# Which early pieces of K and Q take the float32 path through the SP and ACT queues: the third instead of the second

## The chip, the cores and the metric

The kernel runs on one core of a Trainium2 chip. The metric is the device time of one execution in microseconds (us), lower is better; a kernel's time is the median of several runs. Five runs of the kernel before gave 302.68, 302.68, 301.27, 301.18 and 304.01 us.

The engines go by these names: PE is TensorE (matmuls and transposes), ACT is ScalarE, DVE is VectorE, POOL is GpSimd, and SP is SyncE, which only issues transfers. SP and ACT issue transfers through hardware queues (q1 and q10 in the profile), POOL through a software queue (q0), which can change the type of the data on the way.

## The reference

Sliding-window attention over 8 batches of 8 heads, and then a two-layer block with a squared ReLU on all 4608 tokens:

```python
B, H, S, D = 8, 8, 576, 64
scores = (q @ k.T) / sqrt(D)                    # per batch and head, S x S
mask = abs(pos[:, None] - pos[None, :]) <= 32   # window of 32 to both sides
attn = softmax(where(mask, scores, -1e9))
x = (attn @ v), heads side by side              # 4608 x 512
h = x @ w_in                                    # 512 -> 2048
out = (relu(h) ** 2) @ w_out                    # 2048 -> 512, float32
```

Inputs and the output are float32; the kernel computes in bf16 with float32 accumulation.

## The kernel before, in words

**Attention.** Queries go in chunks of 64 tokens (9 for each batch, numbered n = 0 to 71), each against the 128 keys around it. Q and K come in as rows of tokens; PE transposes them against an identity matrix into PSUM, and DVE (K, line 505) and ACT (Q, line 502) copy the result into `KT` and `QT`. Then, for a group of chunks: scores on PE (line 585), the exponential on ACT (605), the mask on DVE (614), attention times V on PE (720 and 721), a reciprocal and a scaling on DVE (731, 733), a transpose of the result on PE (749), and a copy into `XT` on ACT (755). For odd chunks V is needed at another offset, so DVE copies V from `VX` to `VD` (543).

**The block after it.** `mm1` multiplies `XT` by `w_in` (lines 768, 791, 809), ACT applies the ReLU, DVE squares, and `mm2` multiplies by `w_out` (861). The first token tile uses `mm1_small`, which needs 128 tokens and a quarter of `w_in`. The first one needs chunks 0 and 1 in `XT` and the quarter called w10.

**Loading batch 0.** Its tokens come in six pieces, `PIECE0 = ((0, 96), (96, 64), (160, 128), (288, 128), (416, 128), (544, 32))`, as (first token, count). Piece x of K is called k0x here, of Q q0x, of V v0x (V has five pieces of its own). Pieces 0 and 1 of K and Q come by `first_load` (line 454): a plain float32 copy, K on SP's queue and Q on ACT's, into the staging tiles that `STG` names. Piece 0 goes into two of the `OE` tiles, piece 1 into `PF`, 128 partitions of 1040 float32 elements, K at element 0 and Q at element 512. PE transposes them as float32, against a float32 identity `IDF`. All other pieces come by `tok_load` (line 461) on POOL's queue, which casts them to bf16 on the way, and are transposed as bf16. V comes by `vx_load` (531), also on POOL; weights by `load_w1` and `load_w2` (548, 553), on POOL too. The order on POOL's queue is the list `ORDER`, written by hand.

POOL also makes an index pattern with `iota` (line 413). DVE builds the two identities and the masks from it (lines 415 to 426).

**The order on every engine.** The builder records each operation with the tiles that it reads and writes, an assumed duration and a key. A list scheduler in `Prog` orders them by keys and by what an estimate of the course makes of them; keys at or below -100 hold as written. That order is fixed when the program is built, and each engine runs its list strictly in order. A transfer's assumed time is `move`: a count, a time for each, and an allowance at the end.

**Idle matmuls.** Where the scheduler's estimate leaves PE without work in the first part, `fill` puts in matmuls of a zero tile (line 410), which keep PE active; they wait for nothing but must be run through. They stop at `idle_end`, the transposes of piece 3.

The transposes of a piece are in `tok_turn`; which PSUM tiles they use depends on the piece: `HT` (the two tiles of `mm1`) or the score banks B and D.

Of the kernel before, what the change touches and what calls it, by code (L numbers as in the profile page):

```python
# [8 lines left out]
BF16 = mybir.dt.bfloat16  # L9
# [9 lines left out]
VE = D_ + 1  # L19
# [11 lines left out]
PADS, MARGINS, ROUNDS, NREP = (0, 1000, 2000), (0, 4000, 8000), 3, 4  # L31
LATE = {"POOL": 1500, "SP": 2000, "ACT": 2000}
DEPTH, POST, BACK = 4000, {"POOL": 1500, "SP": 1000, "ACT": 1000}, {"POOL": 2500, "SP": 4000, "ACT": 4000}
ORDER = ("v00 v01 k02 q02 v02 w10 k03 q03 v03 k04 q04 v04 w11 w12 w13 k05 q05 k10 q10 v10 k11 q11 v11 "
         "w20 w21 w22 w23 k12 q12 v12 k13 q13 v13 k14 q14 v14").split()
GT0, WT0 = (12.5, 16, 20, 25.5), (13, 18, 23, 26)
TURN0 = {1: 1, 2: 2, 4: 3, 6: 4}
# [321 lines left out]
class Gen:  # L359
# [5 lines left out]
    def alloc(self):  # L365
        nc = self.nc
        sb, ps = nc.alloc_sbuf_tensor, nc.alloc_psum_tensor
        self.SC = ps("sc", [128, 2048], F32)
        self.BK = {x: self.SC[:, 512 * i:512 * i + 512] for i, x in enumerate("ACBD")}
        self.TRP = self.BK["D"].bitcast(BF16)  # L370
        self.HT = [ps(f"ht{i}", [128, 512], F32) for i in range(2)]
        self.OUTP = [ps(f"outp{i}", [128, 512], F32) for i in range(2)]

        self.RAW = {t: [sb(f"{t}raw{i}", [128, 2560], BF16) for i in range(2)] for t in "qk"}
        self.QT = [sb(f"qt{i}", [128, 4, S_], BF16) for i in range(2)]
        self.KT = [sb(f"kt{i}", [128, 4, KW], BF16) for i in range(2)]
        self.VD = [sb(f"vd{i}", [128, 4, H_, VS], BF16) for i in range(2)]
        self.KA = [sb(f"ka{i}", [128, 4, 3, 128], BF16) for i in range(2)]
        self.VX = [sb(f"vx{i}", [128, 5, H_, VS], BF16) for i in range(2)]
        self.MASK = sb("mask", [128, 64], BF16)  # L380
        self.MASK2 = sb("mask2", [128, 2, 64], BF16)
        self.IOTA = sb("iota", [128, 256], mybir.dt.int32)
        self.IDW = sb("identw", [128, 256], BF16)
        self.ID = self.IDW[:, 64:192]
        self.MK = sb("mk", [128, 64], F32)
        self.E = sb("e", [128, 2048], BF16)
        self.PT = sb("pt", [128, 3 * 768], BF16)
        self.RS = [sb(f"rs{i}", [128, 16], F32) for i in range(4)]
        self.XR = sb("xr", [128, 4, 512], BF16)
        self.PF = sb("pf", [128, 16 * VE], F32)  # L390
        self.XT = sb("xt", [128, 4, NTOK], BF16)
        self.W1 = sb("w1", [128, 4, DFF], BF16)
        self.W2 = sb("w2", [128, 16, DM], BF16)
        self.GT = [sb(f"gt{i}", [128, 16, 512], BF16) for i in range(2)]
        self.RT = [sb(f"rt{i}", [128, 512], BF16) for i in range(4)]
        self.ZZ = sb("zz", [128, 128], BF16)
        self.OE = [sb(f"oe{i}", [128, 512], F32) for i in range(4)]
        self.STG = {("k", 0): (self.OE[0], 0, 512, ("oe", 0)), ("q", 0): (self.OE[1], 0, 512, ("oe", 1)),
                    ("k", 1): (self.PF, 0, 16 * VE, ("pf", 0)), ("q", 1): (self.PF, 512, 16 * VE, ("pf", 1))}
        self.IDF = self.OE[3][:, 0:128]  # L400


# [8 lines left out]

    def setup_masks(self, key):
        self.p.rec("POOL", lambda e: e.iota(self.IOTA[:], [[1, 256]], base=0, channel_multiplier=-1), writes=["iota"],
                   key=-198.5, dur=400)
        self.p.rec("DVE", lambda e: e.tensor_scalar(self.IDF, self.IOTA[:, 0:128], 0.0, None, ALU.is_equal),
                   reads=["iota"], writes=[("oe", 3)], key=key - 0.1, dur=200)
        self.p.rec("DVE", lambda e: e.tensor_scalar(self.IDW[:], self.IOTA[:], 64.0, None, ALU.is_equal),
                   reads=["iota"], writes=["id"], key=key, dur=330)
        self.p.rec("DVE", lambda e: e.tensor_scalar(self.MK[:], self.IOTA[:, 0:64], -64.0, None, ALU.is_ge),
                   reads=["iota"], writes=["mk"], key=key + 0.1, dur=130)  # L420
        self.p.rec("DVE", lambda e: e.scalar_tensor_tensor(self.MASK[:], self.IOTA[:, 0:64], 0.0, self.MK[:], ALU.is_le,
                                                           ALU.mult),
                   reads=["mk", "iota"], writes=["mask"], key=key + 0.1, dur=130)
        self.p.rec("DVE", lambda e: e.tensor_scalar(self.MASK2[:, 0, :], self.IOTA[:, 0:64], -64.0, None, ALU.is_le),
                   reads=["iota"], writes=[("mask2", 0)], key=-20, dur=130)
        self.p.rec("DVE", lambda e: e.tensor_scalar(self.MASK2[:, 1, :], self.IOTA[:, 0:64], 0.0, None, ALU.is_ge),
                   reads=["iota"], writes=[("mask2", 1)], key=-20, dur=130)
# [21 lines left out]
    def first_load(self, t, x, eng, key):  # L449
        t0, n = PIECE0[x]  # L450
        src = (self.q if t == "q" else self.k)[0, :, t0:t0 + n, :].rearrange("h p d -> p h d")
        stg, o, w, tag = self.STG[t, x]
        dst = bass.AP(stg, o, [[w, n], [64, 8], [1, 64]])
        self.p.rec(eng, lambda e: e.dma_start(dst, src), writes=[tag], dma=(f"s{t}{x}", 0), key=key, dur=420, move=(n // 2, 14, 1500))

    def tok_load(self, b, t, x, key):
        t0, n = self.pieces(b)[x]
# [8 lines left out]
    def tok_turn(self, b, x, key):  # L466
        t0, n = self.pieces(b)[x]
        early = b == 0 and x < 3
        first = b == 0 and x < 2
        if b == 0 and x == 1:  # L470
            parts = [(t, "s" + u, self.BK[u]) for t, u in ("kB", "qD")]
        elif early:
            parts = [(t, ("ht", u), self.HT[u][:] if first else self.HT[u][:].bitcast(BF16)) for u, t in enumerate("kq")]
        elif b:
            u = "DB"[x % 2]
            ps = self.BK[u].bitcast(BF16)
            parts = [("k", "s" + u, ps[:, 0:512]), ("q", "s" + u, ps[:, 512:1024])]
        elif x == 5:
            parts = [("k", "sD", self.TRP[:, 0:512]), ("q", "sD", self.TRP[:, 512:1024])]
        else:  # L480
            parts = [(t, ("outp", u), self.OUTP[u][:].bitcast(BF16)) for u, t in enumerate("kq")]

        def f(e, todo):
            for t, tag, ps in todo:
                for j in range(4):
                    stg, o, w, _ = self.STG[t, min(x, 1)]
                    src = bass.AP(stg, o + 128 * j, [[w, n], [1, 128]]) if first else bass.AP(
                        self.RAW[t][b % 2], self.slot(b, x) + 128 * j, [[2560, n], [1, 128]])
                    mm = e.transpose(ps[:, 128 * j:128 * j + n], src, self.IDF[0:n, 0:n] if first else self.ID[0:n, 0:n])  # L489
            return mm  # L490

        for todo in ([parts[:1], parts[1:]] if early else [parts]):
            rd = [self.STG[t, x][3] for t, _, _ in todo] + [("oe", 3)] if first else [("fraw", b, t, x) for t, _, _ in todo]
            self.p.rec("PE", lambda e, a=todo: f(e, a), reads=rd + ["id"],
                       writes=sorted({tag for _, tag, _ in todo}), key=key, dur=450 if first else 240 * len(todo), att=True)
        if b == 0 and x == 3:
            self.p.idle_end = self.p.ops[-1]
        for t, tag, ps in parts:
            src = ps[:, 0:512].rearrange("p (j q) -> p j q", j=4)[:, :, 0:n]
            dst = self.KT[b % 2][:, :, 32 + t0:32 + t0 + n] if t == "k" else self.QT[b % 2][:, :, t0:t0 + n]  # L500
            if b == 0 and x < 5 and t == "q":
                self.p.rec("ACT", lambda e, d=dst, c=src: e.activation(d, c, ACTF.Copy), reads=[tag], writes=[(t, b % 2, x)],
                           old=self.was(b, t, x), key=key, dur=200 + 2.8 * n, att=True)
            else:
                self.p.rec("DVE", lambda e, d=dst, c=src: e.tensor_copy(d, c), reads=[tag], writes=[(t, b % 2, x)],
                           old=self.was(b, t, x), key=key, dur=60 + 3.2 * n, att=True)
# [388 lines left out]
    def build(self):  # L895
# [18 lines left out]
        for b in range(B_):  # L914
# [2 lines left out]
                tile += 1  # L917
            if b < FB:
                if not b:
                    for x in range(2):  # L920
                        self.first_load("k", x, "SP", -300 + x)
                        self.first_load("q", x, "ACT", -300 + x)
                for bb in range(0 if b else FB):
# [15 lines left out]
            for c in range(NCH):  # L939
                n = NCH * b + c  # L940
# [33 lines left out]
                if c % 2 and not b:  # L974
                    x = (c + 1) // 2
# [6 lines left out]
                gi, k, m = self.group[n]  # L982
# [48 lines left out]
```

## Time and profile before

| | |
|---|---|
| median of 5 runs | 302.68 us (301.18 to 304.01) |
| the profiled execution's own time | 302.68 us |
| its span in the trace | 300.9 us |
| PE busy | 295.7 us, 98% of the span |
| DVE, ACT, POOL busy | 59%, 53%, 35% |
| POOL's software queue q0 | 114144 packets, 18.03 MB |
| mean granted TensorE clock | 0.994 |

The profile comes from one execution. Its span begins with the first instruction and ends with the last; 1.8 us of the execution's time lie outside of it. Times in it are microseconds from the start of the span. A line number is that of the instruction in the code above. PE and PEld are the two halves of TensorE's work, the streaming of the moving operand and the loading of the stationary one. The granted clock is the share of full speed that the hardware let TensorE run at.

### The profile page before, as it was taken

The numbers are of one execution on the slowest core, as the hardware profiler recorded it, in microseconds if no ns is written. First come the engines' busy times: TensorE is split into PE (matmuls) and PEld (weight loads), VectorE is DVE, ScalarE is ACT, GpSimd is POOL, SyncE is SP. The second block draws the span as 40 slices with busy tenths as digits, with TensorE's granted clock in tenths as the row PEclk, the third lists the DMA queues.
The fourth block names the chain that finished last, engine by engine and source line by source line (L and its number), as shares of the span: only waits on it lengthen the run. The fifth ranks groups of instructions, "written<-read, shape, count | busy, mean of one in ns | idle before, by whom it ended". The sixth has DMA issues, their size and how long they took to land.

```text
span 300.9 us, 7075 instructions
## 1 busy us (share of the span) xinstructions
PE 295.7 (98%) x2793; PEld 174.0 (58%) x2793; DVE 176.8 (59%) x429; ACT 160.1 (53%) x267; POOL 105.9 (35%) x131
## 2 busy tenths in 40 slices
PE   7989999999999999999999999999999999999996
PEld 7879955866768754444444454444444444444445
DVE  6676656764989856757665596768447663222200
ACT  2457644565758645654565665557364554444411
POOL 8999941241615531452154544316410000000000
PEclk9799999999999999999999999999999999999999
DMA  9999999999999999999799999999992210100022
GB/s 139 173 197 170 206 171 191 139 158 188 173 146 141 131 195 133 130 137 160 149 112 127 157 171 158 127 173 90 180 150 77 83 26 35 37 35 36 35 83 93
DMA packets 166817, 39.21 MB, mean 130 GB/s; under 512 B 157824, under 2 KB 162304, under 8 KB 166784
## 3 DMA queue, kind: packets, MB, share of 16 engines
q0 software_dynamic: 114144, 18.03, 88.4%
q1 hardware_dynamic: 46000, 11.02, 24.8%
q10 hardware_dynamic: 6640, 9.70, 10.0%
q8 instruction: 22, 0.36, 0.5%
q14 instruction: 11, 0.09, 0.1%
HBM read 36.70 MB, written 9.44 MB: 153 GB/s over the span
## 4 chain that ended last, share of the span: by engine, by line
PE 96%; DMA 2%; DVE 0%; ACT 0%; issue 0%; SPq 0%
PE outp L861 41%; PE ht L809 28%; PE ht L768 7%; PE ht L791 7%; PE sc L585 4%; PE sc L645 3%; DMA pf<-in_k_dram 2%; PE outp L410 2%; PE sc L489 1%; PE sc L837 1%; PE outp L837 1%; PE sc L720 0%; PE sc L693 0%; PE sc L721 0%; PE outp L749 0%; PE ht L489 0%
## 5 line engine op out<-in xcount | busy, mean ns | idle before, releaser
L861 PE MATMUL outp<-w,gt 128*128 128x512 bf16 x560 | 136.0, 379 | 0.0
L809 PE MATMUL ht<-xt,w 128*128 128x512 bf16 x384 | 94.5, 379 | 0.0
L824 DVE TENSOR_TENSOR gt<-rt 128x512 bf16<-128x512 bf16 x144 | 59.2, 419 | 58.3 <-ACT rt L815 51.1
L815 ACT ACTIVATE rt<-ht 128x512 bf16<-128x512 f32 x96 | 57.3, 598 | 56.8 <-PE ht L809 54.8
L861 PEld LDWEIGHTS outp<-w,gt 128*128 128x128 bf16 x560 | 52.7, 98 | 58.2
L809 PEld LDWEIGHTS ht<-xt,w 128*128 128x128 bf16 x384 | 36.5, 98 | 42.3
L461 POOL DMA_DIRECT2D qraw<-in_q_dram x39 | 34.0, 872 | 50.7 <-PE ht L809 24.4
L461 POOL DMA_DIRECT2D kraw<-in_k_dram x39 | 34.2, 876 | 44.3 <-PE ht L809 19.2
L605 ACT ACTIVATE e<-sc 128x512 bf16<-128x512 f32 (+1 forms) x48 | 37.4, 809 | 12.4 <-PE sc L585 12.4
L531 POOL DMA_DIRECT2D vx<-in_v_dram x40 | 35.2, 879 | 20.6 <-PE ht L809 8.5
L868 ACT ACTIVATE oe<-outp 128x512 f32<-128x512 f32 x35 | 20.9, 598 | 26.6 <-PE outp L861 26.6
L669 DVE TENSOR_TENSOR xr<-pf,rs 128x512 bf16<-128x512 f32 (+1 forms) x42 | 27.7, 682 | 0.4
L626 DVE TENSOR_TENSOR pt<-e,mask 128x512 bf16<-128x512 bf16 x42 | 17.6, 422 | 14.0 <-ACT e L605 13.9
L768 PE MATMUL ht<-xt,w 128*128 128x128 bf16 x384 | 24.1, 219 | 0.3 <-ACT xt L755 0.3
L791 PE MATMUL ht<-xt,w 128*128 128x256 bf16 x192 | 23.5, 273 | 0.0
L768 PEld LDWEIGHTS ht<-xt,w 128*128 128x128 bf16 x384 | 21.7, 98 | 0.8 <-ACT xt L755 0.5
L662 DVE COPY pf<-sc 128x520 f32<-128x520 f32 x21 | 14.7, 699 | 11.6 <-PE sc L645 11.6
L791 PEld LDWEIGHTS ht<-xt,w 128*128 128x128 bf16 x192 | 18.0, 98 | 3.3
L776 ACT ACTIVATE rt<-ht 128x512 bf16<-128x512 f32 x24 | 14.2, 599 | 10.4 <-PE ht L768 10.1
L659 ACT ACTIVATE pf<-sc 128x520 f32<-128x520 f32 x21 | 12.6, 602 | 11.9 <-PE sc L645 11.9
L797 ACT ACTIVATE rt<-ht 128x512 bf16<-128x512 f32 x24 | 14.4, 600 | 7.3 <-PE ht L791 6.8
L664 DVE TENSOR_TENSOR pf<-pf 64x520 f32<-64x520 f32 x21 | 14.6, 697 | 5.9 <-ACT pf L659 4.9
(84 smaller groups left out, 197.2 us busy)
## 6 DMA issues: line engine op xcount, KB each, us to landing
out_dram<-oe ACTq DMA_DIRECT2D x35, 256.0 KB, 3.7
kraw<-in_k_dram POOLq DMA_DIRECT2D x31, 128.0 KB, 5.2
qraw<-in_q_dram POOLq DMA_DIRECT2D x31, 128.0 KB, 5.3
vx<-in_v_dram POOLq DMA_DIRECT2D x24, 128.0 KB, 5.1
w<-in_moe_w_in_dram POOLq DMA_DIRECT2D x4, 512.0 KB, 9.6
w<-in_moe_w_out_dram POOLq DMA_DIRECT2D x4, 512.0 KB, 15.9
vx<-in_v_dram POOLq DMA_DIRECT2D x16, 96.0 KB, 5.6
xt<-xr SPq DMA_TRANSPOSE x36, 4.2
```

Source lines behind the costliest of these rows:

```text
L461: self.p.rec("POOL", lambda e: e.dma_start(dst, src), writes=[("fraw", b, t, x)], old=[("fraw", b - 2, t, y + (b == 2))], reads=self.pace( ...
L531: self.p.rec("POOL", lambda e: e.dma_start(self.VX[b % 2][r:r + n, s, :, 0:64], self.v[b, :, t0:t0 + n, :].rearrange("h p d -> p h d")), w ...
L605: self.p.rec("ACT", lambda e, d=dst, a=src: e.activation(d, a, ACTF.Exp, scale=0.125), reads=["s" + x for x in name], writes=[("e", h)], k ...
L626: self.p.rec("DVE", lambda e, a=pt, c=ee, d=mb: e.tensor_tensor(a, c, d, ALU.mult), reads=[("e", k // 2), "mask"], writes=[("ptt", k)], ol ...
L669: self.p.rec("DVE", lambda e, w=w, np=np: e.tensor_tensor(bass.AP(self.XR, 512 * (2 * y + w), [[2048, np], [64, 2], [128, 4], [1, 64]]), b ...
L768: mm = e.matmul(ht[:, 128 * (d % 4):128 * (d % 4) + 128], self.W1[:, ft, 128 * d:128 * d + 128], self.XT[:, ft, t0:t0 + 128], start=(ft == ...
L791: mm = e.matmul(ht[:, 256 * (d % 2):256 * (d % 2) + 256], self.W1[:, ft, 128 * d:128 * d + 128], self.XT[:, ft, 64 * s0:64 * s0 + 256], st ...
L809: mm = e.matmul(ht[:], self.W1[:, ft, 128 * d:128 * d + 128], self.XT[:, ft, 512 * T:512 * T + 512], start=(ft == 0), stop=(ft == 3))
L815: self.p.rec("ACT", lambda e: e.activation(rt[:], ht[:], ACTF.Relu), reads=[("ht", k % 2)], writes=[("rt", k % 4)], key=key, dur=560)
L824: self.p.rec("DVE", lambda e: e.tensor_tensor(g, r, r, ALU.mult), reads=[("rt", k % 4)], writes=tags, key=key, dur=430)
L861: mm = e.matmul(op, gt[:, d, 128 * u:128 * u + 128], self.W2[:, d, :], start=(d == 0), stop=(d == 15))
L868: self.p.rec("ACT", lambda e: e.activation(oe[:], op, ACTF.Copy), reads=[tag], writes=[("oe", x % 4)], key=key, dur=560)
```

## The change

Piece 2 (128 tokens) takes the place of piece 1 (64 tokens) on the float32 path: `first_load` is called for pieces 0 and 2, and the staging tile `PF` holds piece 2. Piece 1 now comes as bf16 through POOL, and is put first there. The `iota` gets the key of the masks, which sets it ahead of all of POOL's transfers; before, it stood behind the first one (v00). The allowance for the landing of the float32 piece 2 in the scheduler's estimate is 2500 ns instead of 1500 ns.

```diff
-ORDER = ("v00 v01 k02 q02 v02 w10 k03 q03 v03 k04 q04 v04 w11 w12 w13 k05 q05 k10 q10 v10 k11 q11 v11 "
+ORDER = ("k01 q01 v00 v01 v02 w10 k03 q03 v03 k04 q04 v04 w11 w12 w13 k05 q05 k10 q10 v10 k11 q11 v11 "
          "w20 w21 w22 w23 k12 q12 v12 k13 q13 v13 k14 q14 v14").split()
...
         self.STG = {("k", 0): (self.OE[0], 0, 512, ("oe", 0)), ("q", 0): (self.OE[1], 0, 512, ("oe", 1)),
-                    ("k", 1): (self.PF, 0, 16 * VE, ("pf", 0)), ("q", 1): (self.PF, 512, 16 * VE, ("pf", 1))}
+                    ("k", 2): (self.PF, 0, 16 * VE, ("pf", 0)), ("q", 2): (self.PF, 512, 16 * VE, ("pf", 1))}
...
         self.p.rec("POOL", lambda e: e.iota(self.IOTA[:], [[1, 256]], base=0, channel_multiplier=-1), writes=["iota"],
-                   key=-198.5, dur=400)
+                   key=key, dur=400)
...
-        self.p.rec(eng, lambda e: e.dma_start(dst, src), ..., move=(n // 2, 14, 1500))
+        self.p.rec(eng, lambda e: e.dma_start(dst, src), ..., move=(n // 2, 14, 1500 if x == 0 else 2500))
...
-        first = b == 0 and x < 2
+        first = b == 0 and x in (0, 2)
         if b == 0 and x == 1:
-            parts = [(t, "s" + u, self.BK[u]) for t, u in ("kB", "qD")]
+            parts = [(t, "s" + u, self.BK[u].bitcast(BF16)) for t, u in ("kB", "qD")]
...
-                    stg, o, w, _ = self.STG[t, min(x, 1)]
+                    stg, o, w, _ = self.STG[t, x if first else 0]
...
-                    for x in range(2):
+                    for x in (0, 2):
                         self.first_load("k", x, "SP", -300 + x)
                         self.first_load("q", x, "ACT", -300 + x)
```

The scheduler answers with another order at the start. The columns show PE's list up to the transposes of piece 3, "fill" being idle matmuls; from there on PE's list is the same in both.

| before | after |
|---|---|
| 34 fill, transposes k00, 2 fill, q00, 2 fill | 34 fill, transposes k00, 2 fill, q00, 11 fill |
| k01, 2 fill, q01, 2 fill (float32) | scores 0, 1 fill |
| scores 0, 11 fill, scores 1 | k01, 1 fill, q01, 1 fill (bf16) |
| k02 (bf16), av 0, q02 (bf16), 14 fill | k02, q02 (float32), scores 1, av 0, 14 fill |
| av 1, scores 2 and 3, 12 fill | scores 2 and 3, 2 fill, av 1, 15 fill |
| transpose of chunks 0 and 1, 12 fill | transpose of chunks 0 and 1, 2 fill |
| av 2, 2 fill, av 3, 4 fill | av 2, 2 fill, av 3, 11 fill |
| first `mm1_small`, 14 fill, k03, q03 | first `mm1_small`, 18 fill, k03, q03 |

On DVE the copy of k02 stands ahead of the first two V copies (line 543) after the change, where before three V copies stood ahead of it; on ACT the first exponential now stands ahead of the copy of q01, and the copy of q02 ahead of the second exponential.

## Prediction

> **What bounds the kernel now.** I read the chain that ended last first, then PE's waits.
>
> ```profile
> PE 96%; DMA 2%; DVE 0%; ACT 0%; issue 0%; SPq 0%
> PE outp L410 <- DVE zz L404: 1.0, 1, 1.0
> PE sc L489 <- DMA pf<-in_k_dram: 0.8, 1, 0.8
> PE outp L749 <- DVE kt L505: 0.5, 1, 0.5
> PE ht L768 <- ACT xt L755: 0.3, 1, 0.3
> ```
>
> The chain is PE but for one transfer, `pf<-in_k_dram`: k01, which the change touches. The waits (total, times, longest) all lie before 20 us; asked again for 22.3 to 299 us, the view names none. From the scores at 22.27 PE works through a fixed list. So the change is worth what it moves the start of that list by. Next, PE in order of time (start, length), up to there:
>
> ```profile
> 5.44 0.85 PE L489 MATMUL ht<-oe 96*128 96x96 f32 x4
> 7.34 0.46 PE L489 MATMUL sc<-oe,pf 64*128 64x64 f32 x4 [0.84 <-DMA pf<-in_k_dram]
> ...
> 8.56 0.29 PE L585 MATMUL sc<-qt,kt 64*128 64x64 bf16 x8
> ...
> 11.13 1.70 PE L410 MATMUL outp<-zz 128*128 128x128 bf16 x14
> ...
> 16.05 1.06 PE L768 MATMUL ht<-xt,w 128*128 128x128 bf16 x16
> 16.94 0.94 PE L410 MATMUL outp<-zz 128*128 128x128 bf16 x14
> 17.73 0.39 PE L489 MATMUL outp<-identw,kraw 128*128 128x128 bf16 x4
> ```
>
> k01 ends a wait at 7.34; the first `mm1_small` runs at 16.05, k03 is transposed at 17.73. The 14 idle matmuls at 11.13 take 0.107 us each, those at 16.94 0.056. The reason is the granted clock (columns: stretch, length, PE busy, clock, DMA share, GB/s):
>
> ```profile
> 6.38:9.79 3.41, 2.51 (x41) 1.00 2.24 163
> 9.79:13.20 3.41, 3.41 (x46) 0.50 1.77 181
> 13.20:16.60 3.40, 3.40 (x78) 1.00 2.39 161
> ```
>
> Half clock for 3.41 us, right after a stretch in which PE was busy for 2.51 of 3.41 us. Last the transfers: two issues (KB, us to landing), then the packets of 4.0 to 5.4 us, when hardware and software queues share:
>
> ```profile
> pf<-in_k_dram SPq DMA_DIRECT2D x1, 128.0 KB, 6.1
> pf<-in_q_dram ACTq DMA_DIRECT2D x1, 128.0 KB, 4.5
> q0 software_dynamic: 635, 0.08, 92.1%
> q1 hardware_dynamic: 399, 0.10, 56.9%
> q10 hardware_dynamic: 145, 0.03, 19.8%
> ```
>
> The hardware queues move 544 packets in 1.4 us, 389 a us, beside 454 on the software queue. From 6.5 to 8.5 us the software queue alone moves 2391, 1196 a us.
>
> **The change part by part.**
>
> *Scores 0 earlier.* They need only piece 0. k00 and q00 stay: q00's transposes end at 6.08, 11 idle matmuls follow (at half clock until 6.38, then 0.056 each), and scores 0 start at about 6.95 instead of 8.56. This gains nothing by itself: the next output needs scores 1, and these stand behind k02 and q02 in PE's list.
>
> *k01, q01 on POOL.* 512 packets each. At 454 a us from 4.0 they are out by 5.0 and 6.1; v00 took 1.5 us from its last packet to landing at 6.99, so they land near 6.4 and 7.5. Their transposes, four of 64 columns each, end before 8. Without this cover (a later POOL queue) they would cost nothing until 9.9, the next item. The iota ahead puts 0.37 us before k01's issue; with 64 rows instead of v00's 96 the first issue is shorter than the 0.89 us of v00, so the software queue starts within 0.3 us of before. The identities come earlier, but k00 waits for data and idle matmuls until 4.59: 0.
>
> *k02, q02 on SP and ACT.* 128 rows are 1024 packets instead of 512, for each: 1024 more in all before the last lands. k01 landed at 1.19 + 6.11 = 7.30. At 389 a us the additional ones take 2.63 us: k02 lands at 9.93. This is the term that decides. Bounds: at what the hardware queues did while the software queue was silent (576 packets between 3 and 3.5 us, 1152 a us) 8.2; at 300 a us, the thinned end of k01, 10.7. I take 9.93, since POOL has packets queued throughout.
>
> Here the Trainium skill speaks: "DMA: Bandwidth & Descriptors", section "Queues, rings and completion order", has each DMA engine go round-robin over the rows that have work. With SP, ACT and POOL in turn, hardware would get two shares of three of the 843 a us, 562, and k02 land at 7.30 + 1.82 = 9.1. The row speaks against it: SP's k01 reached its rate only as ACT's q01 ran out, and their sum averaged 389 all the same. The rule would make the whole sum 0.8 us smaller.
>
> *PE behind k02.* PE idles from about 8 to 9.97 (it started 0.04 us after the landing before). The stretch before 9.79 is then emptier than the 2.51 us that brought half clock, so I keep half clock until 13.20:
> - eight float32 transposes of 128 columns: q00's 96 columns took 0.160 each at half clock, so 0.213, in all 1.71: to 11.68. Before they were eight in bf16, 0.107 each.
> - scores 1 0.25, av 0 0.46: to 12.39
> - 14 idle matmuls: 7.6 until 13.20, the rest at 0.056: to 13.56; scores 2 and 3 and two idle matmuls: to 14.0.
> - av 1 waits for DVE: k02's copy starts at 11.07 and takes 0.70 (the float32 copies of 256 and 384 elements took 0.42 and 0.56; in bf16 it was 0.42): 11.77. Two V copies (mean of the row 0.42) to 12.61; reciprocal (0.18) after av 0 to 12.84; V copy to 13.28; scaling (0.42) to 13.72; mask of chunk 1 (0.40) to 14.14. av 1 runs to 14.46. Its exponential, behind q02's copy on ACT, is done near 13.1 and hidden by this.
> - 15 idle matmuls to 15.30; meanwhile two V copies to 14.98, reciprocal, scaling to 15.66. Transpose of chunks 0 and 1 to 15.95, two idle matmuls, av 2 behind its mask to 16.40, two more, av 3 to 16.79, 11 idle matmuls to 17.40.
>
> The first `mm1_small` starts at 17.40 instead of 16.05: +1.35. Then 18 instead of 14 idle matmuls, 4 x 0.056 = +0.22. From k03 on the list is the same and each step waits for the one before, so the delay is carried to the end: +1.57.
>
> The clock rule would make this smaller. "TensorE: Matmul & The Clock Gate", Part 1, lets the clock fall after at least one idle window of about 3.4 us; two idle us are less. At full clock k02 and q02 are done 0.7 us earlier, DVE's chain starts 0.4 us earlier, and the sum is about +1.1. But before, 0.9 idle us of 3.41 were enough, so I keep the row.
>
> *Hidden behind the start.* While the hardware queues work 2.63 us longer, POOL's queue loses 742 packets a us, 1950, against 1024 fewer of its own until w10: w10 and all behind land 926 / 1196 = 0.8 us later. w10 landed at 12.4, needed at 17.4; q03 at 15.7, needed at 19.3; w11 at 20.9, needed at 24.2: covered by 2.5 us or more, and without it the excess would be added one to one. v01 lands near 10.1, before DVE asks at 11.77. SP and ACT issue two transfers as before; the longer second issue on ACT stands before a table load that ended 3.1 us before its first use.
>
> The sum is 302.68 + 1.6 = 304.3 us; the profiled execution's time is the median of the runs shown, and its span would go from 300.9 to 302.5.
>
> **The rivals.**
>
> *A few tenths only.* The queues share as the rule has it, k02 lands near 9.1, or the clock stays full. PE's work behind it moves one to one: +0.8, 303.5. For it: hardware queues reached 1152 packets a us alone. Against: the sum of 389. A change below 0.5% (1.5 us) is about what a measurement of this kernel can't tell from none.
>
> *Faster.* k02 lands by 8.3, PE idles so briefly behind the earlier scores 0 that full clock holds through 9.79 to 13.20. Then k02 and q02 are done by 9.35, and DVE's copies decide: mask of chunk 1 at 12.1, first `mm1_small` at 15.35, less 0.7; with V copies at their shortest (0.29) less 1.3. With the +0.22 it is -0.5 to -1.1, 301.6 at best but for the runs' own scatter. It decides only below 8.3, where the hardware queues would have to run as if POOL were silent.
>
> *Slower still.* k02 lands at 10.7, or PE's idle time reaches into the next stretch and half clock lasts to 16.6. The first costs 0.8 more; the second about half of the idle matmuls and av work after 13.2, 1 us. 305.2 to 305.9.
>
> **How the numbers follow.** The forecast with its slower form, over 0.5%, gets 0.48; the few tenths 0.40; faster 0.12. The forecast stands just beyond the limit of 0.5%, so its lower half feeds "same". Range: from 302.0 (the middle between faster and no change) to 305.8 (k02 late).
>
> **What would show it.** Right: `pf<-in_k_dram` some 8.7 us to landing, scores 0 near 7, an idle stretch of PE of 2 us before the float32 transposes near 10, half clock behind it, the first `mm1_small` near 17.4, no PE wait after 24. Wrong: a landing before 9, full clock from 9.8 on, or a first `mm1_small` before 16.

## The result and the profile after

The changed kernel takes 302.28 us (median of 43 runs, 301.90 to 302.86). In 80 runs beside it the kernel before takes 301.22 us (301.02 to 304.01). The ratio, that of the means, is 1.0019, with a 95% interval of 1.0010 to 1.0028: 0.2% slower, below what I had called measurable.

The kernel before can't be read as one number, because its time follows the granted clock. In the runs whose clock is on record it is mostly 301.17 us at a mean of 1.0, 302.67 at 0.994 (one stretch of 3.41 us at half clock, as in the profile shown above) and 304.0 at 0.989. The changed kernel ran at 1.0 in 43 of the 44 runs whose clock is on record. So against the profile that I summed from, 302.68 us, the change gains 0.40 us; against the same kernel at full clock it costs 1.11 us.

The profiled execution of the changed kernel took 302.30 us, its span 300.5 us. First its chain by engine, and PE's waits (total, times, longest):

```profile
PE 94%; DMA 2%; DVE 2%; ACT 0%; issue 0%; POOL 0%; POOLq 0%
```

```profile
PE sc L489 <- DMA kraw<-in_k_dram: 1.1, 1, 1.1
...
PE sc L720 <- DVE pt L614: 0.6, 1, 0.6
...
PE outp L749 <- DVE xr L733: 0.3, 1, 0.3
```

The wait for `pf` is gone. In its place PE waits for `kraw`, which is k01, now on POOL's queue, and then twice for DVE. Before, DVE had no share of the chain; now it has 2%. PE in order of time (start, length, wait in brackets):

```profile
6.50 0.29 PE L585 MATMUL sc<-qt,kt 64*128 64x64 bf16 x8
...
8.07 0.29 PE L489 MATMUL sc<-identw,kraw 64*128 64x64 bf16 x4 [1.12 <-DMA kraw<-in_k_dram]
...
8.76 1.04 PE L489 MATMUL ht<-oe,pf 128*128 128x128 f32 x8
9.74 0.29 PE L585 MATMUL sc<-qt,kt 64*128 64x64 bf16 x8
...
15.43 1.06 PE L768 MATMUL ht<-xt,w 128*128 128x128 bf16 x16
16.33 1.17 PE L410 MATMUL outp<-zz 128*128 128x128 bf16 x18
17.33 0.39 PE L489 MATMUL outp<-identw,kraw 128*128 128x128 bf16 x4
```

Scores 0 start at 6.50, then PE stands still for 1.12 us. The k03 transposes start at 17.33 instead of 17.73: these 0.40 us are the whole difference between the two profiles. The clock (stretch, length, PE busy, granted clock, DMA share, GB/s):

```profile
6.50:9.74 3.24, 2.12 (x29) 1.00 2.25 163
9.74:13.20 3.46, 2.83 (x68) 1.00 1.71 184
13.20:16.60 3.40, 3.12 (x64) 1.00 2.43 158
```

No stretch is at half clock, although PE was busy for only 2.12 of 3.24 us in the first. (These stretches are not the steps in which the clock changes in this run; those stand below, where the prediction's half clock is answered.) The transfers (KB, us from issue to landing):

```profile
pf<-in_k_dram SPq DMA_DIRECT2D x1, 256.0 KB, 5.3
pf<-in_q_dram ACTq DMA_DIRECT2D x1, 256.0 KB, 6.5
...
kraw<-in_k_dram POOLq DMA_DIRECT2D x1, 64.0 KB, 6.7
qraw<-in_q_dram POOLq DMA_DIRECT2D x1, 64.0 KB, 6.3
```

k02, issued at 1.20, lands at 6.47, although it is twice as large as the k01 that SP brought before in 6.1 us. The small k01, issued by POOL at 1.35, lands only at 8.02. The packets of 4.0 to 5.4 us tell why:

```profile
q1 hardware_dynamic: 660, 0.17, 75.1%
q10 hardware_dynamic: 524, 0.13, 60.4%
q0 software_dynamic: 26, 0.00, 3.6%
```

Before, the software queue moved 635 packets in these 1.4 us and the two hardware queues 544. Now it moves 26, and they move 1184, 846 a us. Here is the start of the chain that ended last, as it leads from there to the first `mm1_small` (start, length):

```profile
1.35 6.67 DMA kraw<-in_k_dram
...
8.92 0.46 PE ht L489 x4
...
9.40 0.70 DVE kt L505
...
10.13 0.50 DVE vd L543
...
12.31 0.63 DVE vd L543
...
13.39 0.43 DVE xr L733
```

k01 is late; behind it in PE's list stand k02's float32 transposes, though their data has been there for two microseconds; behind these DVE's copy of k02; behind that the V copies and the scaling that the transpose of chunks 0 and 1 needs.

### The profile page after: what moved, and what is told of

Its sections match the earlier page's. It is cut to its first block, busy times and chain, and to the rows that moved or that the text cites. A ratio compares the mean times of both kernels' runs of the same rounds, so it can differ in the third digit from the quotient of the medians.

```text
span 300.5 us, 7083 instructions
## 1 busy us (share of the span) xinstructions
PE 293.8 (98%) x2796; PEld 171.7 (57%) x2796; DVE 176.1 (59%) x429; ACT 160.1 (53%) x267; POOL 105.5 (35%) x131
## 4 chain that ended last, share of the span: by engine, by line
PE 94%; DMA 2%; DVE 2%; ACT 0%; issue 0%; POOL 0%; POOLq 0%
PE outp L861 41%; PE ht L809 28%; PE ht L791 7%; PE ht L768 7%; PE sc L585 3%; PE sc L645 3%; DMA kraw<-in_k_dram 2%; PE sc L489 1%; PE outp L410 1%; DVE vd L543 1%; PE sc L837 1%; PE outp L837 1%; DVE kt L505 0%; PE sc L693 0%; PE outp L749 0%; DVE pt L614 0%
## 5 line engine op out<-in xcount | busy, mean ns | idle before, releaser
L461 POOL DMA_DIRECT2D qraw<-in_q_dram x39 | 33.2, 853 | 51.7 <-PE ht L809 24.1
L461 POOL DMA_DIRECT2D kraw<-in_k_dram x39 | 33.3, 855 | 43.9 <-PE ht L809 18.4
```

The lines of the kernel that those rows point to most:

```text
L461: self.p.rec("POOL", lambda e: e.dma_start(dst, src), writes=[("fraw", b, t, x)], old=[("fraw", b - 2, t, y + (b == 2))], reads=self.pace( ...
```

## The experiments

My first theory after the result: the hardware queues hold the software queue back while they have packets, so 1024 more packets on them delay everything on POOL. Its rival: POOL's own order, the iota and k01 ahead, moves the start of the software queue. Two more questions go with it: whether the ratio depends on how often the kernel before is at half clock, and whether an idle gap of PE is what brings half clock. Times "at full clock" are those of runs with a mean granted clock of 0.999 or 1.0.

**The kernel before, twice more.** No edit.

> The kernel before, unchanged, profiled again. In the profile shown, TensorE had half clock from 9.79 to 13.20 us and the time was 302.68 us; most runs of it give about 301.18. Theory: those are runs at full clock, with the first mm1_small near 14.6 and k03 transposed near 16.2, and everything else as in the trace shown. Rival: the 1.5 us lie elsewhere, in the transfers, and k01 lands earlier than 7.30.

> The kernel before once more, for a profile at full clock, which the two profiles so far were not. If it falls into clock 1.0 (about half of its runs): the time is 301.2 us, the first mm1_small comes near 14.6 and k03 is transposed near 16.2, and PE's idle matmuls before av 1 take 0.056 us each. If it falls into 0.994 again, this run tells nothing new.

302.86 us and 302.70 us, both profiled at a clock of 0.994. There is no profile of the kernel before at full clock; where this text says how it looks then, it uses the last experiment. The half clock lies elsewhere in each: 0.51 from 9.79 to 13.20 in the first; in the second 0.78 from 6.38 to 9.79 and 0.72 from 9.79 to 13.20, which is 3.41 us from 8.30 on.

**The iota alone ahead**, in the kernel before:

```diff
-                   key=-198.5, dur=400)
+                   key=key, dur=400)
```

> The kernel before with only the iota put ahead of v00. Theory A (the hardware queues hold the software queue back while both have work): the first packet of the software queue comes at 3.6 us as before, k01 lands near 7.3, and the time is that of before within 0.1%. Theory B (the software queue starts late in the changed kernel because of what stands ahead in it, the iota and a short first load): the first packet moves from 3.6 towards 5.0 us.

301.51 us (22 runs), ratio 0.9983 (0.9963 to 1.0003). The most common time, at full clock, is 301.50, 0.33 over the 301.17 before; fewer runs are at half clock (5 of 22 below 0.999, against 38 of 51 of the kernel before beside it). The theory that only the number of hardware packets matters had the software queue start unchanged, and that missed: its packets up to 4.5 us fell from 268 to 5 (first the kernel before),

```profile
q0 software_dynamic: 268, 0.03, 12.2%
```

```profile
q0 software_dynamic: 5, 0.00, 0.2%
```

while SP's k01 landed at 6.34 instead of 7.30. POOL's first issue starts only 0.10 us later here (1.40 instead of 1.30), its second even 0.27 us earlier (2.29 instead of 2.56); in this one profile that was enough for the hardware queues to go first. So the rival has a part: the order on POOL shifts the race too. That the profiled run is no faster for an earlier k01 lies in DVE's V copies (line 543): the first five take 3.18 us instead of 1.96. What they wait for is told below.

**128 rows in the hardware loads, nothing else**, in the kernel before (the 64 added rows are not used):

```diff
-        t0, n = PIECE0[x]
+        t0, n = PIECE0[x][0], 96 if x == 0 else 128
...
-move=(n // 2, 14, 1500))
+move=(PIECE0[x][1] // 2, 14, 1500))
```

> The kernel before, but the second transfer of K on SP and of Q on ACT brings 128 rows instead of 64; the 64 added rows go to free partitions of the staging tile and are not used. All orders stay. Theory A: the software queue's first packet moves from 3.6 to about 5.0 us, v00 lands near 8.4 instead of 7.0, k02 on POOL near 9.5 instead of 8.4; k01 on SP lands no later than 7.5, since the hardware queues run at up to 850 packets a us while the software queue is silent. Theory B: first software packet at 3.6 us, and the hardware packets thinned by it, so that k01 on SP lands near 9.9.

302.56 us (12 runs), ratio 1.0007 (0.9982 to 1.0032); at full clock it is 302.55, 1.4 over the kernel before at full clock. Packets of 4.0 to 5.4 us:

```profile
q1 hardware_dynamic: 771, 0.19, 82.7%
q10 hardware_dynamic: 442, 0.11, 51.4%
q0 software_dynamic: 36, 0.00, 5.0%
```

```profile
pf<-in_k_dram SPq DMA_DIRECT2D x1, 256.0 KB, 5.5
```

With POOL's list as before, the picture is that of the changed kernel: the hardware moves 866 packets a us, the software queue 36 in all. k01, carrying twice the packets, lands at 6.70, earlier than the 7.30 before. This shows the first theory at the place in dispute.

**64 rows in the changed kernel's hardware loads** (the upper half of k02 and q02 is zeros from a memset on DVE):

```diff
+        t0, n = PIECE0[x][0], 96 if x == 0 else 64
...
+        self.ms("DVE", ["pfz"], self.PF[64:128, 0:1024], 0.0, K + 1, 500)
```

> The changed kernel with only 64 of the 128 rows of piece 2 sent through SP and ACT; the other 64 partitions are zeros set by VectorE, so half of piece 2 is left out of the result. The orders of PE, ACT and POOL are those of the changed kernel. Theory A: the software queue's first packet comes near 3.6 us again and k01 lands near 6.6 instead of 8.0; then k02 or q02 on the hardware queues, near 7.3, is what PE waits for, and the first mm1_small comes 0.6 us or more earlier than the 15.43 of the changed kernel. Theory B: the software queue starts at 5.0 us as in the changed kernel and nothing is gained.

The profiled run took 301.30 us. Its packets of 4.0 to 5.4 us, and its k01:

```profile
q0 software_dynamic: 638, 0.08, 89.2%
q1 hardware_dynamic: 393, 0.10, 48.7%
q10 hardware_dynamic: 238, 0.06, 26.5%
```

```profile
kraw<-in_k_dram POOLq DMA_DIRECT2D x1, 64.0 KB, 5.4
```

With POOL's list exactly that of the changed kernel, the software queue is back at 638 packets, k01 lands at 6.79 instead of 8.02, the first `mm1_small` starts at 14.36 instead of 15.43, and k03 at 16.26 instead of 17.33. So beside this trace the additional hardware packets cost 1.07 us; beside the second profile of the changed kernel (k03 at 16.96) it is 0.70. Over all runs it is less clear: at full clock there are nine of 301.28 to 301.32 and nine of 302.71 to 302.73, and two of 304.31 at 0.994; median 302.71, ratio 0.9988 (0.9965 to 1.0011). No run of the upper group was profiled, so what separates the two groups is open.

In this pair of runs the number of packets and the form of the transfer change together. With 64 rows SP's queue almost stands still from 3.4 to 4.2 us (19 packets before, 30 here), and the software queue starts in this gap; with 128 rows SP's queue moves 501 there in the run above and 569 in the changed kernel. Whether the number or the form closes the gap, no run separates.

**The changed kernel again**, in a later set of runs.

> The changed kernel again, beside runs of the kernel before on this chip. Theory C (the sign depends on how often the kernel before gets a half-clock stretch in its first 20 us): this kernel runs at granted clock 1.0 in nearly every run and takes 302.3 us; the kernel before takes 301.2 at clock 1.0, 302.7 at 0.994 and 304.0 at 0.989, so the ratio lies anywhere from 1.004 to 0.998 by the mixture. Rival: this kernel falls into half clock as often as the other, and its own time spreads over 302.3, 303.8 and 305.

301.98, 302.30, 302.32 and 302.70 us at full clock, 304.28 at 0.994. Beside it 22 of 35 runs of the kernel before were at full clock, with a median of all of 301.35, and the ratio is 1.0045 (1.0022 to 1.0068). Beside the first experiments only 13 of 51 were, and the median was 302.69; against that, 302.3 us would be 0.999. So the sign of the difference depends on how often the kernel before is throttled.

The profiled run, 301.98 us, shows how far the changed kernel's own race differs from run to run: k02 lands at 6.55, but k01 at 7.64 instead of 8.02, PE waits for it 0.52 us instead of 1.12, and the software queue moves 63 packets from 4.0 to 5.4 us instead of 26.

**k02 ahead of k01 in PE's list**, in the changed kernel. Two allowances of the scheduler's estimate change; it then puts k02's transposes ahead of scores 0, q02's behind them, and k01 and q01 after that:

```diff
-move=(n // 2, 14, 1500 if x == 0 else 2500))
+move=(n // 2, 14, 1500 if x == 0 else 1000))
...
-move=(n // 2, 13.3, (0, 500, 800, 800, 800, 800)[x] if b == 0 else 200))
+move=(n // 2, 13.3, (0, 1000, 800, 800, 800, 800)[x] if b == 0 else 200))
```

> The changed kernel with other assumed landing times for piece 1 and piece 2, by which the scheduler puts the transposes of k02 and q02 (which land at 6.5 and 7.7 us) ahead of those of k01 and q01 (8.0 and 8.4). If what the changed kernel pays for is the late landing of k01 with the float32 transposes queued behind it on PE, scores 1 come at about 9.2 instead of 9.7 us, and the time is 301.8 instead of 302.3. If k01's landing alone sets it, the time stays at 302.2 to 302.4.

301.58 us (20 runs, all at full clock; 12 near 301.5, 8 near 302.67), ratio 1.0007 (0.9991 to 1.0022). The profiled run, 301.59 us, has k03 at 16.69, against 17.33 and 16.96 in the two profiles of the changed kernel. The k02 transposes start at 6.67, 2.1 us earlier, and the gap before k01 is filled with work that has its data. So the order that PE's list has in the changed kernel, made for a late k02 and an early k01, costs time, since the transfers came the other way round: 0.7 us by the medians, 0.27 to 0.64 by the profiles. The eight runs near 302.67 are slower than the changed kernel's 302.28; none was profiled, and what holds them back is open.

**Ten idle matmuls ahead of k01**, in the kernel before:

```diff
+ (10 if op is self.more else 0)
...
+        if b == 0 and x == 1:
+            self.p.more = self.p.ops[-2]
```

> The kernel before with ten more idle matmuls ahead of the transposes of k01, where PE waits 0.8 us for its transfer. Theory D (the half clock comes from this gap): the granted clock is 1.0 in nearly all runs and the time is 301.2 us in nearly all; ratio 0.995 to 1.000 by how often the kernel before is throttled. Rival: the clock falls for another reason, the runs spread over 301.2, 302.7 and 304 as before, and the additional idle matmuls cost 0 to 0.3 us.

301.57 us (301.08 to 301.91, 13 runs, all at full clock), ratio 0.9997 (0.9981 to 1.0012). PE is busy for 3.16 us of the stretch instead of 2.51:

```profile
6.38:9.79 3.41, 3.16 (x43) 1.00 2.26 165
9.79:13.20 3.41, 3.33 (x76) 1.00 1.74 179
```

The half clock is gone in all runs. The median is still 0.4 over the kernel before at full clock, and not because of the ten: in the profiled run, 301.91 us, PE had run through them and waited another 0.25 us. There k01 itself came later, its transposes starting at 7.65 instead of 7.34 (7.25 with five idle matmuls), and DVE's first five V copies took 2.53 us, against 1.96 with five. Whether this holds for the other runs is not known.

**14 instead of 18 idle matmuls ahead of k03**, in the changed kernel:

```diff
+ - (4 if op is self.idle_end else 0)
```

> The changed kernel with 14 instead of 18 idle matmuls between the first mm1_small and the transposes of k03. If these four lie on the path, as the prediction's term of 0.22 us has it, the time is 302.05 us at full clock instead of 302.28. If the transposes of k03 wait for their transfer or another engine there, nothing changes.

302.07, 302.43 and 302.45 us at full clock, 304.01 and 304.64 at 0.994; ratio 1.0059 (1.0031 to 1.0086). It doesn't settle the 0.22 us: the three runs at full clock show no gain, and two of five were throttled. That the four idle matmuls guard the clock doesn't follow: in the profiled run the half clock starts at 15.01, ahead of their place, after DVE's slow V copies (five in 2.99 us) had kept PE waiting.

**The changed kernel with the iota behind its first transfer**, as before the change:

```diff
-                   key=key, dur=400)
+                   key=-198.5, dur=400)
```

> The changed kernel with the iota behind POOL's first transfer, as in the kernel before; nothing else differs. Theory A (the 1024 additional packets on the hardware queues hold the software queue back): its first packet still comes near 5 us, k01 lands near 8 and the time stays at 302.0 to 302.5 us at full clock. Theory B' (the iota ahead delays the software queue, as it did by 0.6 us in the kernel before): the first packet comes near 4.4, k01 lands 0.6 us earlier, and the time is about 301.7.

302.98 us (20 runs, 15 at full clock), ratio 1.0058 (1.0043 to 1.0073). k01 lands at 7.66 and scores 1 start at 9.35, as in the second profile of the changed kernel (7.64 and 9.34), so no gain shows there. Still it is 0.7 us slower than the changed kernel, which no theory had foreseen. DVE's V copies, first in this kernel, then in the changed one:

```profile
9.74 1.19 DVE L543 COPY vd<-vx 64x528 bf16<-64x528 bf16 x2
...
12.52 1.42 DVE L543 COPY vd<-vx 64x528 bf16<-64x528 bf16 x2
```

```profile
10.13 0.83 DVE L543 COPY vd<-vx 64x528 bf16<-64x528 bf16 x2
...
12.31 0.95 DVE L543 COPY vd<-vx 64x528 bf16<-64x528 bf16 x2
```

Two pairs of copies take 1.19 and 1.42 us instead of 0.83 and 0.95, and a fifth copy 0.54 instead of 0.30: 1.07 us more on DVE's part of the chain, less the 0.38 us by which k02's copy starts earlier (9.02 against 9.40), leaves 0.69. The first `mm1_small` is 0.66 later (16.09). So the place of the loss in this profile is shown. What such a copy waits for can be read from POOL's issues beside it, first a slow copy in this kernel, then a quick one in the kernel before:

```profile
9.84 0.97 POOL L461 DMA_DIRECT2D qraw<-in_q_dram  x1
10.09 0.84 DVE L543 COPY vd<-vx 64x528 bf16<-64x528 bf16 x1
```

```profile
6.93 0.94 POOL L461 DMA_DIRECT2D kraw<-in_k_dram  x1
7.08 0.29 DVE L543 COPY vd<-vx 64x528 bf16<-64x528 bf16 x1 [0.66 <-DMA vx<-in_v_dram]
```

The slow copy ends 0.12 us after the end of the issue in which it began. The first five copies of all 13 profiles, 65 in all, fall into two kinds. 43 take 0.32 to 0.85 us, and each ends 0.09 to 0.13 us after its issue. The other 22 take 0.29 to 0.30 us; they began in the first 0.24 us of an issue or in its last 0.19. POOL issues back to back through the whole stretch in every version. All five wait here and two in the first profile of the changed kernel, but all five wait in the profile with 14 idle matmuls too, where the iota is ahead. So the loss comes from how the copies fall against POOL's issues; that the iota's place makes them fall badly in most runs is an inference. The Trainium skill ("SBUF — State Buffer", "SBUF: two separate sides") says that VectorE, in some of its modes, and GpSimd share a pair of ports which one locks for a whole instruction. The wait for the end of the issue agrees with it, the copies that get through in the first 0.24 us of one do not; and no run took the issues away.

**Five idle matmuls ahead of k01**, in the kernel before: the same edit as the ten, with 5.

> The kernel before with five instead of ten additional idle matmuls ahead of k01. With ten no run of 13 was throttled and the median was 301.57 us, 0.4 above the full-clock runs of the kernel before. If the ten lie partly on the path, five give 301.2 to 301.4 at full clock; if the gap left open is long enough, some runs fall to 0.994 and 302.7 again.

301.27 us (22 runs, 21 of them at full clock, one of 304.04 at 0.989). The kernel before took 301.44 beside it, with 26 of 43 runs at full clock. The ratio on record is 0.9975 (0.9959 to 0.9992); the quotient of the means is 0.9987.

```profile
6.38:9.79 3.41, 2.70 (x44) 1.00 2.16 165
9.79:13.20 3.41, 3.30 (x73) 1.00 1.74 176
```

```profile
7.25 0.46 PE L489 MATMUL sc<-oe,pf 64*128 64x64 f32 x4 [0.71 <-DMA pf<-in_k_dram]
...
14.53 1.06 PE L770 MATMUL ht<-xt,w 128*128 128x128 bf16 x16
...
16.20 0.39 PE L489 MATMUL outp<-identw,kraw 128*128 128x128 bf16 x4
```

The five end well before k01 lands (0.71 us of waiting are left), so they cost nothing, and they bring the full-clock time nearly always. This is the one version whose interval lies wholly below the kernel before, and its gain is the absence of half clock: at full clock alone its median is 301.25, against 301.18.

## Why the prediction was wrong

It said 304.3 us, by +1.57 against the profiled run; measured was 302.28, -0.40 against that run and +1.11 against the kernel before at full clock. By its steps:

- *Scores 0 earlier*: right. They started at 6.50 (said 6.95), helped by a full clock from 3.91 on instead of 6.38, and it gained nothing by itself.
- *k02 lands at 9.93*: this step failed, and it decided the sum. The measured landing is 6.47. I took the 389 packets a us that the hardware queues moved beside a busy software queue as their rate whenever POOL has packets queued. But while SP's and ACT's queues are both busy, the software queue moves almost nothing. In the profile before, one of the two was always nearly idle: SP's from 3.4 to 4.2 us (19 packets), when the software queue moved its first 150, and ACT's from 4.2 to 5.4 (82 packets), when it moved 550. My lower bound of 8.2 was no bound either: it was added to 7.30, a landing that was itself delayed by the sharing. The Trainium skill's round-robin ("DMA: Bandwidth & Descriptors", "Queues, rings and completion order"), which I had weighed there, is not what the runs show: with transfers issued on all three rows, the software row got 26 of 1210 packets.
- *k01 and q01 on POOL, hidden*: failed with it. k01 lands at 8.02 instead of 6.4, and is the new wait, 1.12 us. The 0.37 us that I gave the iota did not do this: POOL's first issue starts at 1.35 instead of 1.30, and with the iota behind it k01 still lands at 7.66. I costed the transfer by the software queue's rate before and never asked what 1024 more packets on the hardware queues would do to it. I had named a delay of POOL's later transfers (0.8 us, hidden; it was 0.36 for w10, 12.76 against 12.40, and hidden) but not of its first.
- *Half clock kept to 13.20*: failed. The changed kernel ran at full clock, here and in all but two of the 49 runs whose clock is on record. Even with k02 landing late this term was a throw: the kernel before itself has half clock in some runs and not in others. Where a trace records a change of the clock, it comes in steps of 3.41 us from a start that differs by run: full clock begins at 6.38 in the profile before, at 3.91 in the changed kernel, at 4.89 in the last profile of the kernel before, at 4.77 with 14 idle matmuls. The Trainium skill ("TensorE: Matmul & The Clock Gate", Part 1) calls the window of the clock gate free-running, which agrees with that. Cut along these steps, PE's busy time is (stretch, length, PE busy, clock, DMA share, GB/s; the changed kernel, then the last profile of the kernel before, then the one with 14 idle matmuls):

```profile
3.91:7.33 3.42, 2.78 (x39) 1.00 1.73 189
7.33:10.74 3.41, 2.67 (x44) 1.00 1.93 179
```

```profile
4.89:8.30 3.41, 1.78 (x20) 1.00 2.45 156
8.30:11.72 3.42, 3.42 (x45) 0.50 1.57 192
```

```profile
11.60:15.01 3.41, 1.53 (x29) 1.00 2.33 160
15.01:18.43 3.42, 3.42 (x44) 0.50 1.89 181
```

The changed kernel's gap of 1.12 us, from 6.95 to 8.07, was divided between two steps, neither of them as empty as those before a fall. In the four profiles with a half clock the step before it had PE busy for 1.53, 1.78, 2.33 and 2.51 us. An idle window, which the page asks for before the fall, no run shows. Nor is PE's busy share alone the rule: steps with 2.34 us (4.77 to 8.19 with 14 idle matmuls) and 2.42 us (8.90 to 12.31 with the iota behind) brought none, and 2.50 us (10.74 to 14.15) none in the changed kernel.
- *From k02's copy to the first `mm1_small`*: right in mechanism and nearly in size. I had 11.07 to 17.40, 6.33 us; measured is 9.40 to 15.43, 6.03. The float32 copy took 0.70, as estimated, and DVE did become what PE waits for.
- *Four more idle matmuls, 0.22*: they take 0.056 us each (18 in 1.00). That leaving them out would gain this was not shown.
- *Carried one to one*: right. From the start of k03's transposes to the end it is 283.2 us before (300.9 - 17.73), after (300.5 - 17.33) and with the five idle matmuls (299.4 - 16.20).

The error adds up: k02's transposes start 1.21 us earlier than predicted (8.76 against 9.97), full clock saves 0.46 on the way to DVE's copy (0.64 against 1.10), and DVE's part is 0.30 shorter. 1.21 + 0.46 + 0.30 = 1.97, and 1.57 - 1.97 = -0.40.

The nearest story was the rival *Faster*: k02 landing below 8.3 and full clock, first `mm1_small` at 15.35. Both conditions came, and it started at 15.43. I had given it 0.12, since hardware queues "would have to run as if POOL were silent". They did; they are what silences it. That the two starts agree within 0.1 us is luck in part: the story had no wait for k01.

One error lies ahead of all steps. The five times shown before, 301.18, 301.27, 302.68, 302.68 and 304.01, were three modes of one kernel, and I summed against a run of the middle one because it was the median. Against the mode at full clock the same events are a loss: scores 1 at 9.74 instead of 9.46 (the latter from the kernel with five idle matmuls), the first `mm1_small` 0.90 later, and four idle matmuls more make k03 1.13 later. Against the middle mode they are a gain of 0.40.

## What to carry to other kernels

Where several queues load at once, don't take one queue's rate from a stretch in which another was running dry: look at packets by queue in short windows, and ask of a transfer that is enlarged whom it holds back, not only how long it takes itself. When the times of one kernel come in steps, find the step of the profiled run before summing against it. And where a list is fixed by assumed landing times, check the order in which the transfers really land: here k02 came 1.5 us before k01, and the list waited for k01.

## What the runs showed of the hardware

- The software queue gives way to the hardware queues: from 4.0 to 5.4 us it moved 26 to 63 packets in the six profiles with 1024 more hardware packets, and 572 to 705 in the seven others. Its first packet came at 4.5 to 5.1 us in the six, at 3.6 to 4.2 in the others.
- A few idle matmuls decide the clock: five in one gap, 2.70 instead of 2.51 us busy in 3.41, and throttled runs went from 17 of 43 to 1 of 22. The clock changed in steps of 3.41 us whose start differs from run to run. What exactly the gate measures stays open.
- A bf16 copy of 64 x 528 elements on DVE takes 0.29 us, or it waits for the end of the transfer issue that POOL is in, up to 0.85 us in all: 43 of 65 copies waited so.
